# Local attention: sums of q k on VectorE, products p v on ScalarE, order of issue planned anew

## The chip, the core and the metric

The kernel runs on 1 core of one Trainium2 chip. The metric is the device time of one execution in microseconds (us). TensorE is PE in the profile's rows (PEld its weight loads), VectorE is DVE, ScalarE is ACT, GpSimd is POOL, SyncE is SP; SP and POOL issue the DMAs here (rows with a q, as SPq, are an engine's queue).

## The reference

B, H, S, D = 8, 8, 576, 64. Attention is computed twice, once on q, k, v averaged over groups of 4 tokens and repeated, once within a band of 7 neighbours; the sum goes through two matrices gated with each other, and two more matrices:

```
out_d = softmax(scale * mean4(q) mean4(k)^T) mean4(v)      # 144 x 144 per head
out_up = repeat(out_d, 4)
scores = where(|i - j| < 4, scale * q k^T, -1e9)
x = out_up + softmax(scores) v                             # 4608 tokens x 512
h = (x w1 * x w2) w3                                        # 512 -> 1024 -> 1024
out = h w_out                                               # 1024 -> 512
```

All in float32, the weights wider. TensorE works with each factor split into a high and a low float32r part, three matmuls for one product.

## The kernel before

*Work on TensorE.* `fold` multiplies w3 by w_out once (`accw`, line 408) and keeps it as `wphl`. Then come 12 chunks of 384 tokens (`moe`): for each of 8 features f two gates (`pab`, 12 matmuls each, lines 323 to 325), a copy by ScalarE (`a`, 1010), a product by VectorE (1012), a split in `gh` (ScalarE, 1017) and `gl` (VectorE, 1019), and `down` (`acc`, 9 matmuls with `wphl`). Only two banks hold `pab`, so TensorE stops when `a` comes late. Pooled attention (`pooled`, `quad`: `s_ps`, `t_ps`, `o_ps`) is spread between. The local attention of the first two batches goes through TensorE as well (`group_unit`).

*Local attention of the other six batches.* It is 18 units (`unit`), each half a chunk, 192 tokens: on 128 partitions (8 heads times 16 blocks of 36 tokens) 12 tokens of 64 elements each, 768 elements. For each of 7 offsets o, VectorE multiplies q by shifted k (`pr`, 863) and the 64 elements of each token are summed into `s_t` (by VectorE in one instruction, 876, or by ScalarE token by token, 873, two instructions each). After a softmax of small instructions, `s_t` multiplies shifted v into `pv` (VectorE, one instruction, 930, or ScalarE, 12 instructions, 922), and the seven `pv` are added into `xl` (VectorE, 940, or a DMA that adds, issued by POOL, 938). A transpose (944), the pooled part (951) and the split (957, 958) end the unit; two units make a chunk's `xh` and `xl`.

*Buffers.* `q_t` has one buffer (`q=1` in `BUFS`), `pr` three, `pv` three. k and v share three buffers `kv`; k of a unit, v of it, and so on take them in turn, so that k of a unit takes the buffer of v of two units before. The loads of `q_t` (842), k (846) and v (850) are issued by SyncE, in one queue with the pooled loads and the stores of `o_sb` (1039, 1041).

*Who does what.* `SHARE` sets it, by offset o, and for the added DMAs by place i in the order of adding:

```
SHARE = dict(qk_pool=(), qk_act=(2, 4), av_act=(3, 5), dma_add=(2, 4, 6))
others = [o for o in range(W) if o in share["av_act"]]
mine = [o for o in range(W) if o not in others]
while mine or others:
    order += mine[:1] + others[:1]
```

*Order.* Nothing runs where it is written. Each step is recorded by `add(engine, cost, ...)` with what it needs; `Plan.order` lists all steps from these costs (`dve_us`, `act_us`, `mm_us` and numbers in place), then shifts priorities by the tables `SHIFTS`, and the steps are emitted in that order, each engine working in order. A cost is a number for the planner alone, not a wait.

Of the kernel before, what the change touches and what calls it, by code (L numbers as in the profile page):

```python
# [15 lines left out]
ALU = mybir.AluOpType  # L16
# [6 lines left out]
SD = S // FAC  # L23
# [29 lines left out]
BUFS = dict(pr=3, pv=3, xl=2, xt=1, q=1, kv=3, w3=5, early_raw=4, early_wx=2, late_raw=3, late_wx=2, a=2,
            g=2, o=2, ab=2, acc=1, ps=3, p=1, pt=1, oup=2, vs=1, qks=1, x=2, s=3, gs=3, q4=2, k4=2, qn=2, vw=4, se=4, pte=1, xf=1)


SHARE = dict(qk_pool=(), qk_act=(2, 4), av_act=(3, 5), dma_add=(2, 4, 6))
# [9 lines left out]
AHEAD = 4  # L67

SHIFTS = [
    "gates.8.2:2 gates.9.5:-15.5",  # L70
    "down.0.1:-10 down.0.4:21.5 down.0.5:47.5 down.0.7:-65 down.1.1:-12 down.1.5:2 down.11.2:-4.5 down.2.0:-1"
    " down.2.2:-2 down.2.3:-11.5 down.2.4:-7.5 down.2.5:-46.5 down.3.2:-14.5 down.3.3:8.5 down.3.6:-11"
    " down.3.7:-29.5 down.4.4:-7 down.4.6:-10 down.5.4:14 down.6.4:-36 down.6.5:5 down.6.6:2.5 down.6.7:-52"
    " down.7.4:-19 down.7.7:1.5 down.8.4:3.5 down.8.5:74 down.9.2:3 down.9.3:-24 gate_block.0.0.0:-5.5"
    " gate_block.0.1.0:-21 gate_block.0.1.1:-15.5 gate_block.1.0.2:-20.5 gate_block.1.1.0:-26.5"
    " gate_block.1.1.2:-6.5 gates.0.0:-14 gates.0.1:-4 gates.0.2:-3.5 gates.0.5:-6 gates.1.1:1 gates.1.3:2"
    " gates.1.6:-2.5 gates.2.0:4.5 gates.2.1:-11.5 gates.2.2:2.5 gates.2.3:-3 gates.2.4:-3 gates.2.5:0.5"
    " gates.3.1:-7 gates.3.2:-30 gates.3.5:-31 gates.3.7:-16.5 gates.4.0:-20.5 gates.4.1:-29 gates.4.2:-14"
    " gates.4.4:1.5 gates.5.2:3.5 gates.5.3:0.5 gates.5.6:-3 gates.5.7:-1.5 gates.6.0:2 gates.6.2:-19.5 gates.6.3:-2"
    " gates.6.6:-1 gates.7.1:1.5 gates.7.6:-0.5 gates.8.3:2.5 gates.8.7:3 gates.9.6:-31.5 group_scores.0.2.0:4"  # L80
    " group_scores.0.2.1:3.5 group_scores.1.0.1:4.5 group_scores.1.1.0:-3 group_values.1:-14 group_values.2:3"
    " out_weight.3:-1 out_weight.4:3 out_weight.6:14 part.6.1:10.5 pooled.0:2.5 pooled.1:4.5 pooled.3:5.5"
    " pooled.4:3.5 pooled.6:11 pooled_sums.1:2.5 product.4.5:-6 product.7.0:7 product.7.1:4 quad.1.0:10.5"
    " quad.2.0:-6 quad.2.1:1 quad.3.0:-4.5 quad.3.1:-1 quad.4.0:1.5 quad.4.1:1 quad.6.0:0.5 quad.7.0:-7.5 rest.0:-1"
    " rest.1:-21.5 unit.11:-1 unit.13:1 unit.14:1 unit.16:1 unit.17:-4.5 unit.20:0.5 unit.21:2 unit.22:-0.5"
    " unit.23:7 unit.6:-1 unit.7:-0.5",
]

LOWS = dict(early=('ACT', 'ACT', 'DVE'), late=('ACT', 'DVE'))
# [176 lines left out]
def dve_us(n, fast=False):  # L266
    return n / 1920 + 0.155 if fast else n / 960 + 0.1
# [8 lines left out]


def mm_us(n):
    return n * 0.43e-3 + 0.0095


SWITCH = 0.19
# [2 lines left out]
def dma_us(n, add=False):  # L285
    return n / (180e3 if add else 320e3)
# [3 lines left out]
def tile_attention_moe(ctx: ExitStack, tc: tile.TileContext, q, kw, vw, qk4, v4, w1, w2, w3, wout, edge, out):  # L290
    nc = tc.nc
# [17 lines left out]
    soft = wpool.tile([128, 3, KEYS[2] + SD], F32, name="pexp")  # L309
# [5 lines left out]
    gates = [[wpool.tile([128, KT, 2, 512], F32R, name=f"w{w}a"), None, None] for w in (1, 2)]  # L315
# [15 lines left out]
    early, late = [], []  # L331
# [221 lines left out]
    def quad(b, qd, P, lq, hq, hpt):  # L553
# [32 lines left out]
            ex.append(e)  # L586

        t1 = add("DVE", 0.19, lambda: nc.vector.tensor_scalar(out=T["rs"][:, :nt], in0=T["sm"][:, :nt], scalar1=1e-9, scalar2=float(FAC), op0=ALU.add, op1=ALU.mult), ex, uses=[hg])
        rs = add("DVE", 0.12, lambda: nc.vector.reciprocal(T["rs"][:, :nt], T["rs"][:, :nt]), [t1], uses=[hg])
        no = []  # L590
        wide_ = lambda x, n: x.unsqueeze(2).to_broadcast([128, nt, n])
        width = (SD, 128)
        if b in PB:
            for par, i in slots:
                no.append(add("ACT", act_us(SD, 1), lambda par=par, i=i: nc.scalar.mul(out=T["of"][par][:, i, :width[par]], in_=T["of"][par][:, i, :width[par]], mul=T["rs"][:, i, par:par + 1]), [rs], uses=[hg, hp]))
        else:
            for par in range(2):
# [33 lines left out]
    @plan.named  # L631
    def pooled_sums(b):

        fours[b], four_ready[b] = {}, []
        hq, done = None, []
        for qd in range(2):
            fours[b][qd] = {}
            tq = hn = None
            for w in range(2):
                x = {}  # L640

                def load_q(qd=qd, w=w, x=x):
# [24 lines left out]
                done.append(t)
                pep.extend([lq4, tq])

            def load_k(qd=qd):  # L670
                x = fours[b][qd][1] = pools["pep"].tile([128, FAC, 2, SD], F32, name="k4", bufs=BUFS["k4"])
                for f in range(FAC):
                    nc.sync.dma_start(out=x[:, f], in_=qk4[b, f, :, 1, 2 * qd:2 * qd + 2])
            lk4, hk4 = add("SP", 2.0, load_k, take=[R["k4"]], late=dma_us(128 * 4608))
            t = lk4
            for f in range(1, FAC):
                def total(qd=qd, f=f):
                    to, x = raws[b][0][:, 1, 2 * qd:2 * qd + 2], fours[b][qd][1]
# [155 lines left out]
    def unit(n):  # L834
# [74 lines left out]
        for i, o in enumerate(order):  # L909
# [266 lines left out]
```

## Time and profile before

| | us |
|---|---|
| median of 3 runs | 773.48 (770.54 to 774.76) |
| profiled execution, its own time | 773.75 |
| its span | 771.9 |
| granted TensorE clock, mean | 0.994 |
| busy: PE / DVE / ACT / POOL | 739.4 / 618.3 / 525.5 / 153.2 |
| instructions | 14990 |

The span runs from the first to the last instruction of the profiled execution; matmuls overlap, so the sum of their durations is over PE's busy time. Waits are put down to what released the instruction last. The rows that matter are shown in the prediction.

### The profile page before, as it was taken

What the parts mean: (1) busy time and instruction counts of PE and PEld (TensorE: products, weight loads), DVE (VectorE), ACT (ScalarE), POOL (GpSimd) and SP (SyncE); (2) the same over time, 40 slices, a digit from 0 to 9 for tenths busy, and PEclk for the clock granted to TensorE, in tenths of its full rate; (3) what the DMA queues carried; (4) which work ended last, traced back from release to release, by engine and by line L of the source; (5) the groups of instructions that cost most, each with busy time, mean ns of one, the idle gap of its engine ahead of it and who ended that gap; (6) DMA issues with size and microseconds to landing.
All of it is one profiled execution on the core that took longest, in us unless ns stands there. A gap on an engine that the chain in (4) does not pass through costs nothing.

```text
span 771.9 us, 14990 instructions
## 1 busy us (share of the span) xinstructions
PE 739.4 (96%) x5248; PEld 640.1 (83%) x5248; DVE 618.3 (80%) x1076; ACT 525.5 (68%) x2074; POOL 153.2 (20%) x187
## 2 busy tenths in 40 slices
PE   3899989999999999999999999999999999999994
PEld 1345578789988999899998898999988998999994
DVE  5658886658999999999997999999989999973110
ACT  4679688547877787867787688677686886742211
POOL 1120033101012512141130422420223320110000
PEclk9999999999999999999999999999999999999998
DMA  9995768415349747877459668764569544331101
GB/s 313 307 285 168 229 176 202 86 42 186 68 115 239 148 109 210 165 147 174 106 132 209 99 158 221 135 169 110 124 150 224 121 100 123 80 65 20 42 1 41
DMA packets 46051, 111.91 MB, mean 145 GB/s; under 512 B 6280, under 2 KB 12424, under 8 KB 45976
## 3 DMA queue, kind: packets, MB, share of 16 engines
q0 software_dynamic: 15360, 38.94, 29.6%
q1 hardware_dynamic: 30616, 72.01, 28.6%
q8 instruction: 41, 0.67, 0.4%
q14 instruction: 34, 0.28, 0.1%
HBM read 80.26 MB, written 9.44 MB: 116 GB/s over the span
## 4 chain that ended last, share of the span: by engine, by line
PE 75%; DMA 9%; DVE 7%; ACT 5%; issue 3%; POOL 0%; SPq 0%; DVEq 0%; ACTq 0%; POOLq 0%
PE pab L323 15%; PE pab L325 15%; PE pab L324 15%; PE acc L323 7%; PE acc L325 7%; PE acc L324 7%; DMA raw<-in_w_dram 4%; DMA kv<-in_kw_dram 2%; DMA out_dram<-o_sb 2%; PE accw L408 2%; DVE pr L863 2%; PE o_ps L527 1%; PE s_ps L566 1%; PE t_ps L609 1%; DMA xl<-pv 1%
## 5 line engine op out<-in xcount | busy, mean ns | idle before, releaser
L873 ACT ACTIVATE junk<-pr 128x64 f32<-128x64 f32 x432 | 111.2, 257 | 23.8 <-DVE pr L863 12.8
L863 DVE TENSOR_TENSOR pr<-q_t,kv 128x768 f32<-128x768 f32 x126 | 119.6, 967 | 3.9 <-DMA kv<-in_kw_dram 3.5
L922 ACT ACTIVATE pv<-kv,s_t 128x64 f32<-128x64 f32 x432 | 111.0, 338 | 12.1 <-DVE s_t L899 6.5
L323 PE MATMUL acc<-wphl,gh 128*128 128x512 f32 x288 | 114.4, 397 | 0.0
L325 PE MATMUL acc<-wphl,gl 128*128 128x512 f32 x288 | 113.2, 393 | 0.9 <-DVE gl L1019 0.9
L324 PE MATMUL acc<-wphl,gh 128*128 128x512 f32 x288 | 112.7, 391 | 0.0
L938 POOL DMA_DIRECT2D xl<-pv x54 | 48.4, 896 | 300.5 <-DVE xl L940 211.8
L1010 ACT COPY a<-pab 128x384 f32<-128x384 f32 x96 | 45.8, 477 | 70.5 <-PE pab L325 54.7
L1012 DVE TENSOR_TENSOR a<-pab,a 128x384 f32<-128x384 f32 x96 | 53.1, 553 | 48.4 <-PE pab L325 46.4
L876 DVE TENSOR_REDUCE s_t<-pr 128x12 f32<-128x768 f32 x90 | 84.1, 946 | 0.4
L873 ACT ACTIVATION_READ_ACCUMULATOR junk<-pr 128x1 f32 x432 | 81.2, 188 | 0.0
L1017 ACT CAST gh<-a 128x384 fp32r<-128x384 f32 x96 | 48.9, 509 | 45.1 <-PE acc L324 38.9
L1019 DVE TENSOR_TENSOR gl<-a,gh 128x384 fp32r<-128x384 f32 x96 | 54.2, 566 | 27.5 <-ACT gh L1017 25.9
L408 PE MATMUL accw<-wo,w 128*128 128x512 f32 x128 | 62.1, 621 | 14.4 <-DVE w L370 13.3
L930 DVE TENSOR_TENSOR pv<-kv,s_t 128x768 f32<-128x768 f32 x72 | 69.6, 969 | 0.1
L323 PE MATMUL pab<-xh,wb 128*128 128x384 f32 x192 | 66.1, 344 | 2.1 <-ACT a L1010 2.1
L323 PE MATMUL pab<-xh,w1a 128*128 128x384 f32 x192 | 65.9, 343 | 2.1 <-ACT a L1010 1.6
L323 PE MATMUL pab<-xh,wo 128*128 128x384 f32 x192 | 65.9, 343 | 0.3 <-ACT a L1010 0.3
L323 PE MATMUL pab<-xh,w2a 128*128 128x384 f32 x192 | 65.2, 340 | 0.5 <-DVE a L1012 0.5
L325 PE MATMUL pab<-xh,wb 128*128 128x384 f32 x192 | 65.2, 339 | 0.0
L324 PE MATMUL pab<-xl,wb 128*128 128x384 f32 x192 | 65.2, 339 | 0.0
L324 PE MATMUL pab<-xl,w1a 128*128 128x384 f32 x192 | 64.9, 338 | 0.3
(117 smaller groups left out, 1717.2 us busy)
## 6 DMA issues: line engine op xcount, KB each, us to landing
xl<-pv POOLq DMA_DIRECT2D x54, 384.0 KB, 4.3
raw<-in_w_dram SPq DMA_DIRECT2D x32, 512.0 KB
qks<-in_qk_dram POOLq DMA_DIRECT2D x18, 576.0 KB, 7.3
kv<-in_kw_dram SPq DMA_DIRECT2D x18, 576.0 KB
kv<-in_vw_dram SPq DMA_DIRECT2D x18, 576.0 KB
q_t<-in_q_dram SPq DMA_DIRECT2D x18, 384.0 KB
out_dram<-o_sb SPq DMA_DIRECT2D x24, 256.0 KB
raw<-in_wout_dram SPq DMA_DIRECT2D x8, 512.0 KB
```

The lines of the kernel that those rows point to most:

```text
L323: nc.tensor.matmul(out_ps, lhsT=lh, rhs=rh, start=first, stop=False)
L324: nc.tensor.matmul(out_ps, lhsT=lh, rhs=rl, start=False, stop=False)
L325: nc.tensor.matmul(out_ps, lhsT=ll, rhs=rh, start=False, stop=last)
L408: nc.tensor.matmul(accs[m], lhsT=T["x"][:, j % 4 * 128:j % 4 * 128 + 128], rhs=wo[0][:, j], start=j == 0, stop=j == NF - 1)
L863: (nc.gpsimd if o in share["qk_pool"] else nc.vector).tensor_tensor(out=T[o], in0=T["q"], in1=T["k"][:, o * D:o * D + nq].rearrange("p (t ...
L873: nc.scalar.activation(out=junk, in_=T[o][:, t], func=AF.Copy, accum_out=T["s"][:, t, o:o + 1])
L876: reds.append(add("DVE", dve_us(nq), lambda o=o: nc.vector.tensor_reduce(out=T["s"][:, :, o], in_=T[o], op=ALU.add, axis=AX.X), [tp], uses ...
L922: nc.scalar.mul(out=T["pv", o][:, tt], in_=T["v"][:, (tt + o) * D:(tt + o + 1) * D], mul=T["s"][:, tt, o:o + 1])
L930: nc.vector.tensor_tensor(out=T["pv", o], in0=T["v"][:, o * D:o * D + nq].rearrange("p (t d) -> p t d", d=D), in1=T["s"][:, :, o].unsqueez ...
L1012: tg = add("DVE", dve_us(CT), lambda f=f: nc.vector.tensor_tensor(out=T["a", f], in0=T["p", 1, f], in1=T["a", f], op=ALU.mult), [ta, ends[ ...
L1017: nc.scalar.copy(out=T["gh", f], in_=T["a", f])
L1019: tl = add("DVE", dve_us(CT), lambda f=f: nc.vector.tensor_tensor(out=T["gl", f], in0=T["a", f], in1=T["gh", f].bitcast(F32), op=ALU.subtr ...
```

## The change

Per unit, VectorE takes all seven sums of q k (ScalarE did those of o = 2 and 4). Of the seven products p v ScalarE takes five (o = 1, 2, 3, 5, 6; before 3 and 5), VectorE two (0 and 4). Two adds go by DMA instead of three, at places 2 and 5, so VectorE adds four instead of three. `q_t` gets a second buffer. Some costs of the planner change, and the tables that shift the order are new, so all engines' orders are.

```
-BUFS = dict(pr=3, pv=3, xl=2, xt=1, q=1, kv=3, ...
+BUFS = dict(pr=3, pv=3, xl=2, xt=1, q=2, kv=3, ...
-SHARE = dict(qk_pool=(), qk_act=(2, 4), av_act=(3, 5), dma_add=(2, 4, 6))
+SHARE = dict(qk_pool=(), qk_act=(), av_act=(1, 2, 3, 5, 6), dma_add=(2, 5))
 SHIFTS = [
-    "gates.8.2:2 gates.9.5:-15.5",
+    "group_scores.0.1.0:-3",
...
 def mm_us(n):
-    return n * 0.43e-3 + 0.0095
+    return n * 0.432e-3 + 0.0098
...
-        rs = add("DVE", 0.12, lambda: nc.vector.reciprocal(...
+        rs = add("DVE", 0.16, lambda: nc.vector.reciprocal(...
-                no.append(add("Pool", 0.18 + nt * width[par] * 2.4e-3, ...
+                no.append(add("Pool", 0.32 + nt * width[par] * 2.4e-3, ...
-        no.append(add("DVE", dve_us(nt * KR), ...
+        no.append(add("DVE", dve_us(nt * KR) + 0.17, ...
-                    tq, hn = add("DVE", dve_us(4 * SD), turn, ...
+                    tq, hn = add("DVE", 0.58, turn, ...
-                    t = add("Pool", 0.9, lambda o=o: nc.gpsimd.dma_start(out=T["x"], in_=T["pv", o], accum_op=ALU.add), ...
+                    t = add("Pool", 0.83, lambda o=o: nc.gpsimd.dma_start(out=T["x"], in_=T["pv", o], accum_op=ALU.add), ...
```

Lines behind the shift tables stand one line higher in the changed kernel. Three places of the order follow; numbers behind names are those of the buffers' tiles.

SyncE's queue at the tenth local unit (the one whose k load the trace shows at 407 us). Before: its q is `q_t_5016`, its k `kv_5047`, its v `kv_5054`; `vs` and `vl` are loads of the pooled v.

```order
L1041 DMA out_0_dram<-o_sb_4907 8x16x512
L1041 DMA out_0_dram<-o_sb_4957 4x16x512 x2
L1041 DMA out_0_dram<-o_sb_4997 8x16x512
L842 DMA q_t_5016<-in_q_dram 128x768
L846 DMA kv_5047<-in_kw_dram 128x1152
L850 DMA kv_5054<-in_vw_dram 128x1152
L490 DMA vs_5112<-in_v4_dram 72x512
L491 DMA vs_5112<-in_v4_dram 56x512
L492 DMA vl_5113<-in_v4_dram 16x512
```

After: its k is `kv_5166`, its v `kv_5172`; `q_t_5125` is the q of the eleventh unit.

```order
L1040 DMA out_0_dram<-o_sb_4950 8x16x512
L1040 DMA out_0_dram<-o_sb_4974 4x16x512 x2
L1040 DMA out_0_dram<-o_sb_5015 8x16x512
L841 DMA q_t_5125<-in_q_dram 128x768
L489 DMA vs_5138<-in_v4_dram 72x512
L490 DMA vs_5138<-in_v4_dram 56x512
L491 DMA vl_5139<-in_v4_dram 16x512
L845 DMA kv_5166<-in_kw_dram 128x1152
L849 DMA kv_5172<-in_vw_dram 128x1152
```

The load of q moved one unit ahead; k and v of the unit moved behind the pooled v.

ScalarE's queue at the products of the eighth local unit, whose v gives up the buffer for that k. Before: v is `kv_4403`, and VectorE's product `pv_5035` is the last one that reads it.

```order
L922 ACTIVATE pv_4773<-kv_4403,s_t_4488 128x64 x6
L922 ACTIVATE pv_4841<-kv_4403,s_t_4488 128x64 x6
L581 ACTIVATE pexp_77,gsm_4807<-s_ps_4809,gnb_4806 128x144 x3
L581 ACTIVATE pexp_77,gsm_4807<-s_ps_4810,gnb_4806 128x144
L1017 CAST gh_4874<-a_4771 128x384
L581 ACTIVATE pexp_77,gsm_4807<-s_ps_4810,gnb_4806 128x144 x2
L1010 COPY a_4888<-pab_4790 128x384
L922 ACTIVATE pv_4841<-kv_4403,s_t_4488 128x64 x4
L1028 COPY o_sb_4907<-acc0_4371 128x512
L922 ACTIVATE pv_4841<-kv_4403,s_t_4488 128x64 x2
L873 ACTIVATE junk_74,s_t_4800<-pr_4877 128x64 x2
```

After: v is `kv_4451`, `pv_5120` is the fifth product of ScalarE.

```order
L921 ACTIVATE pv_5033<-kv_4451,s_t_4553 128x64 x6
L615 COPY pt_4856<-t_ps_5036 128x6x64
L615 COPY pt_4856<-t_ps_5040 128x6x64
L617 COPY pt_4856<-t_ps_5044 128x12x16
L921 ACTIVATE pv_5033<-kv_4451,s_t_4553 128x64 x6
L921 ACTIVATE pv_5120<-kv_4451,s_t_4553 128x64 x8
L539 COPY oup_5144<-o_ps_5086 128x2x9x16
L539 COPY oup_5144<-o_ps_5091 128x2x9x16
L921 ACTIVATE pv_5120<-kv_4451,s_t_4553 128x64 x4
L1016 CAST gh_5161<-a_4909 128x384
L890 ACTIVATE s_t_4870<-s_t_4870 128x84
```

The last reader of v moved from VectorE to ScalarE, up to the exponential (890) of the next unit.

VectorE's queue where the first local unit begins. Before (products `pr`, sums `s_t`; 1019 and 1012 belong to the gates):

```order
L863 TENSOR_TENSOR pr_2290<-q_t_2237,kv_2221 128x768
L876 TENSOR_REDUCE s_t_2289<-pr_2290 128x12
L863 TENSOR_TENSOR pr_2315<-q_t_2237,kv_2221 128x768
L863 TENSOR_TENSOR pr_2326<-q_t_2237,kv_2221 128x768
L1019 TENSOR_TENSOR gl_2313<-a_2268,gh_2312 128x384
L863 TENSOR_TENSOR pr_2339<-q_t_2237,kv_2221 128x768
L1012 TENSOR_TENSOR a_2328<-pab_2319,a_2328 128x384
L876 TENSOR_REDUCE s_t_2289<-pr_2315 128x12
```

After:

```order
L862 TENSOR_TENSOR pr_2265<-q_t_2214,kv_2212 128x768
L875 TENSOR_REDUCE s_t_2264<-pr_2265 128x12
L862 TENSOR_TENSOR pr_2283<-q_t_2214,kv_2212 128x768
L862 TENSOR_TENSOR pr_2291<-q_t_2214,kv_2212 128x768
L1011 TENSOR_TENSOR a_2281<-pab_2274,a_2281 128x384
L862 TENSOR_TENSOR pr_2300<-q_t_2214,kv_2212 128x768
L875 TENSOR_REDUCE s_t_2264<-pr_2283 128x12
L875 TENSOR_REDUCE s_t_2264<-pr_2291 128x12
L875 TENSOR_REDUCE s_t_2264<-pr_2300 128x12
```

Each `pr` is now summed by VectorE. From the first `pr` to the second `xl` split (958, now 957), which completes the first chunk of local units, VectorE's queue holds 72 instructions of 768 elements before and 79 after.

More of the change, by code (lines that the diff above doesn't have):

```diff
@@ L50 @@
 NG = UN // GQ
[L53 removed]
+BUFS = dict(pr=3, pv=3, xl=2, xt=1, q=2, kv=3, w3=5, early_raw=4, early_wx=2, late_raw=3, late_wx=2, a=2,
             g=2, o=2, ab=2, acc=1, ps=3, p=1, pt=1, oup=2, vs=1, qks=1, x=2, s=3, gs=3, q4=2, k4=2, qn=2, vw=4, se=4, pte=1, xf=1)
[L57 removed]
+SHARE = dict(qk_pool=(), qk_act=(), av_act=(1, 2, 3, 5, 6), dma_add=(2, 5))
 TOKENS = 2
@@ L69 @@
 SHIFTS = [
-    "gates.8.2:2 gates.9.5:-15.5",
[L71 to L86, printed above, removed]
[16 rows of a table added]
 ]
@@ L588, in quad @@
         t1 = add("DVE", 0.19, lambda: nc.vector.tensor_scalar(out=T["rs"][:, :nt], in0=T["sm"][:, :nt], scalar1=1e-9, scalar2=float(FAC), op0=ALU.add, op1=ALU.mult), ex, uses=[hg])
-        rs = add("DVE", 0.12, lambda: nc.vector.reciprocal(T["rs"][:, :nt], T["rs"][:, :nt]), [t1], uses=[hg])
+        rs = add("DVE", 0.16, lambda: nc.vector.reciprocal(T["rs"][:, :nt], T["rs"][:, :nt]), [t1], uses=[hg])
         no = []
@@ L597, in quad @@
             for par in range(2):
-                no.append(add("Pool", 0.18 + nt * width[par] * 2.4e-3, lambda par=par: nc.gpsimd.tensor_tensor(out=T["of"][par][:, :, :width[par]], in0=T["of"][par][:, :, :width[par]], in1=wide_(T["rs"][:, :nt, par], width[par]), op=ALU.mult), [rs], uses=[hg, hp]))
-        no.append(add("DVE", dve_us(nt * KR), lambda: nc.vector.tensor_tensor(out=soft[:, :nt, KEYS[1]:KEYS[2]], in0=T["of"][1][:, :, 128:], in1=wide_(T["rs"][:, :nt, 1], KR), op=ALU.mult), [rs], uses=[hg, hp]))
+                no.append(add("Pool", 0.32 + nt * width[par] * 2.4e-3, lambda par=par: nc.gpsimd.tensor_tensor(out=T["of"][par][:, :, :width[par]], in0=T["of"][par][:, :, :width[par]], in1=wide_(T["rs"][:, :nt, par], width[par]), op=ALU.mult), [rs], uses=[hg, hp]))
+        no.append(add("DVE", dve_us(nt * KR) + 0.17, lambda: nc.vector.tensor_tensor(out=soft[:, :nt, KEYS[1]:KEYS[2]], in0=T["of"][1][:, :, 128:], in1=wide_(T["rs"][:, :nt, 1], KR), op=ALU.mult), [rs], uses=[hg, hp]))
         pts = []
@@ L651, in pooled_sums @@
                 if w == 0:
-                    tq, hn = add("DVE", dve_us(4 * SD), turn, [lq4], take=[R["qn"]], uses=[hq4])
+                    tq, hn = add("DVE", 0.58, turn, [lq4], take=[R["qn"]], uses=[hq4])
                 else:
-                    tq = add("DVE", dve_us(4 * SD), turn, [lq4, tq], uses=[hq4, hn])
+                    tq = add("DVE", 0.58, turn, [lq4, tq], uses=[hq4, hn])
                 t = lq4
@@ L937, in unit @@
                 if i in share["dma_add"]:
-                    t = add("Pool", 0.9, lambda o=o: nc.gpsimd.dma_start(out=T["x"], in_=T["pv", o], accum_op=ALU.add), [t, tm], uses=[hx, h], late=dma_us(128 * nq * 4, True))
+                    t = add("Pool", 0.83, lambda o=o: nc.gpsimd.dma_start(out=T["x"], in_=T["pv", o], accum_op=ALU.add), [t, tm], uses=[hx, h], late=dma_us(128 * nq * 4, True))
                 else:
```

15 rows, old and new, of the table SHIFTS are left out of this document.

## The prediction

> **What bounds the kernel now.** I read the page's busy shares first, then busy time by stage, then the waits and the chain of waits inside the one stage where something stops, and last the groups of instructions that the change touches.
>
> ```profile
> PE 739.4 (96%) x5248; PEld 640.1 (83%) x5248; DVE 618.3 (80%) x1076; ACT 525.5 (68%) x2074; POOL 153.2 (20%) x187
> ...
> 0.00:60.00 60.00, 44.99 (x233) 19.58 (x233) 34.56 (x86) 37.12 (x83) 11.25 (x28) 1.00 0.95 304
> 60.00:180.00 120.00, 115.66 (x1425) 89.67 (x1424) 89.18 (x221) 87.16 (x295) 19.94 (x23) 1.00 0.58 157
> 180.00:680.00 500.00, 496.63 (x3171) 454.99 (x3170) 470.63 (x735) 381.05 (x1653) 119.48 (x133) 1.00 0.63 144
> 680.00:760.00 80.00, 80.00 (x417) 74.51 (x416) 23.98 (x37) 18.40 (x42) 2.58 (x3) 1.00 0.12 25
> 760.00:771.90 11.90, 2.08 (x10) 1.38 (x8) 0.00 (x0) 1.76 (x3) 0.00 (x0) 0.77 0.24 66
> ```
>
> After each stretch and its length stand the busy times of PE, PEld, DVE, ACT and POOL, then granted clock, DMA share and GB/s. PE is the bound. What it lacks of the span is 32.5 us: 15.0 in the first 60 us, where the DMA share is 0.95; 4.3 from 60 to 180; 3.4 in the whole of 180 to 680, where the local attention runs; nothing from 680 to 760; 9.8 in the tail. The change keeps all 5248 matmuls, so it can gain only by taking stops of PE away. VectorE, at 470.6 of 500 us in the local stage, is next: when it stops, PE soon does.
>
> The waits of PE from 180 to 680 are two rows, and the longest piece has a chain that can be read in order of time:
>
> ```profile
> PE pab L323 <- ACT a L1010: 2.3, 3, 1.8
> PE acc L325 <- DVE gl L1019: 0.9, 1, 0.9
> ...
> 404.99 1.75 DVE pr L863 x2
> ...
> 406.76 0.66 SPq L842
> ...
> 407.47 15.15 DMA kv<-in_kw_dram
> ...
> 407.47 2.48 SPq L846 DMA_DIRECT2D kv<-in_kw_dram  x1
> ...
> 422.71 0.96 DVE L863 TENSOR_TENSOR pr<-q_t,kv 128x768 f32<-128x768 f32 x1 [3.49 <-DMA kv<-in_kw_dram]
> ...
> 426.29 0.45 DVE gl L1019
> ...
> 426.76 0.49 ACT a L1010
> ...
> 427.29 0.44 PE pab L323
> ```
>
> Unit by unit: the last product of a unit (404.99) frees the only `q_t`; SyncE, in order, issues the next `q_t` (406.76), only then `kv` with k; k takes 15.15 us, VectorE stops 3.49 us in front of its next product, `gl` and `a` are late, PE stops 1.8 us. It costs more than the stop:
>
> ```profile
> 425.00:428.00 3.00, 1.16 (x6) 0.74 (x6) 3.00 (x6) 1.24 (x4) 1.63 (x3) 1.00 0.67 127
> 428.00:431.00 3.00, 3.00 (x13) 3.00 (x12) 3.00 (x5) 1.95 (x9) 2.27 (x3) 0.59 0.63 80
> 431.00:434.00 3.00, 3.00 (x16) 3.00 (x15) 2.53 (x5) 2.81 (x16) 0.90 (x2) 0.84 0.37 57
> ```
>
> 1.84 us idle, then a granted clock of 0.59 and 0.84: 3 x 0.41 + 3 x 0.16 = 1.7 us of matmul time lost. One such stop is worth 3.5 us. The Trainium skill, TensorE: Matmul & The Clock Gate, What's actually happening, says the clock falls back after an idle window of about 3.4 us; by it a stop of 1.84 us costs 1.84 and no more. The trace differs: 0.59 after 1.84 us.
>
> **The change part by part.** There are 18 local units. These groups carry it (busy us, mean ns of one):
>
> ```profile
> L863 DVE TENSOR_TENSOR pr<-q_t,kv 128x768 f32<-128x768 f32 x126 | 119.6, 967 | 3.9 <-DMA kv<-in_kw_dram 3.5 <-ACT junk L873 0.4
> L873 ACT ACTIVATE junk<-pr 128x64 f32<-128x64 f32 x432 | 111.2, 257 | 23.8 <-DVE pr L863 12.8
> L922 ACT ACTIVATE pv<-kv,s_t 128x64 f32<-128x64 f32 x432 | 111.0, 338 | 12.1 <-DVE s_t L899 6.5 <-DMA xl<-pv 5.3
> L876 DVE TENSOR_REDUCE s_t<-pr 128x12 f32<-128x768 f32 x90 | 84.1, 946 | 0.4
> ...
> 402.72 0.55 DVE L1012 TENSOR_TENSOR a<-pab,a 128x384 f32<-128x384 f32 x1
> 403.19 0.94 DVE L876 TENSOR_REDUCE s_t<-pr 128x12 f32<-128x768 f32 x1
> ...
> 406.65 1.80 DVE L876 TENSOR_REDUCE s_t<-pr 128x12 f32<-128x768 f32 x2
> 408.38 0.94 DVE L930 TENSOR_TENSOR pv<-kv,s_t 128x768 f32<-128x768 f32 x1
> 409.24 0.96 DVE L944 STREAM_TRANSPOSE xt<-xl 128x768 f32<-128x768 f32 x1
> ...
> 402.06 0.26 ACT L873 ACTIVATE junk<-pr 128x64 f32<-128x64 f32 x1
> 402.22 0.19 ACT L873 ACTIVATION_READ_ACCUMULATOR junk<-pr 128x1 f32 x1
> 402.44 0.26 ACT L873 ACTIVATE junk<-pr 128x64 f32<-128x64 f32 x1
> ...
> 415.18 1.55 ACT L922 ACTIVATE pv<-kv,s_t 128x64 f32<-128x64 f32 x6
> ```
>
> Instructions overlap, so I cost them from start to start: a wide VectorE instruction of 768 elements 0.87 us (two reduces from 406.65 to 408.38; product 408.38 to 409.24), one of 128x384 0.47 (402.72 to 403.19), a sum of one token on ScalarE 0.38 (402.06 to 402.44), a product of one token 0.24 ((1.55 - 0.34) / 5).
>
> - VectorE: two more sums per unit, +36 x 0.87 = +31.3; three products fewer (of five), -54 x 0.87 = -47.0; adds four instead of three, +18 x 0.87 = +15.7. Sum 0.0.
> - ScalarE: -432 x 0.38 = -164.2, +648 x 0.24 = +155.5. Sum -8.7. It is idle a third of the span; worth nothing by itself.
> - POOL and DMA: adds by DMA go from 54 to 36.
>
> ```profile
> q0 software_dynamic: 15360, 38.94, 29.6%
> q1 hardware_dynamic: 30616, 72.01, 28.6%
> ...
> xl<-pv POOLq DMA_DIRECT2D x54, 384.0 KB, 4.3
> ```
>
> 18 x 384 KB = 7.1 of the 38.9 MB of q0, 18% of its 29.6%: the DMA share of the span falls by 5.4 points. No engine waits for bytes on average; it counts only where a load lands late.
>
> - `q_t` in two buffers: a load no longer waits for the last product of the unit just ahead of its own. But in the new order each `q_t` load stands one unit earlier, so the last product of a unit still gates the `q_t` load that SyncE has ahead of the next k; behind that wait stand k and v of the next unit and, at some units, the pooled v. The 3 KB per partition that it needs cost no time.
> - k's own buffer: with three buffers in the ring k and v take turns, and k of a unit takes the buffer that v of two units before gives up. VectorE's last product gave it up before; now ScalarE's twelfth token of the fifth product does, shortly ahead of use.
>
> The sum, stage by stage. At the stop of 425 the issue of k ended at 407.47 + 2.48 = 409.95, and VectorE could have used it at 422.71 - 3.49 = 419.2, 9.3 us later. In the new order, at the same unit, between ScalarE's last token of the freeing product and the first product stand on VectorE 7 wide instructions, 4 of 128x384 and four small: 6.1 + 1.9 = 8.0, some 9 with the small. That is the same lead, on queues with 5 points less on them. Between all of the stop staying (0) and all of it going (-3.5) I take the middle: -1.8. The other PE stops of the stage:
>
> ```profile
> 300.00:360.00 60.00, 59.65 (x379) 54.04 (x378) 55.89 (x89) 45.05 (x189) 18.75 (x21) 1.00 0.77 170
> 560.00:600.00 40.00, 38.84 (x271) 34.35 (x270) 36.45 (x61) 29.92 (x126) 13.37 (x16) 1.00 0.81 184
> ...
> 570.88 7.69 DMA xl<-pv
> ```
>
> 0.35 + 1.16 = 1.5 us, the larger one behind an add by DMA that took 7.69 us. With a third fewer adds, in less traffic, I take two thirds away: -1.0 (between 0 and -1.5).
>
> A new place is the first chunk that the local units feed. Up to its second `xl` the new order puts 79 wide instructions on VectorE where there were 72, +7 x 0.87 = +6.1 us, because sums that ScalarE did beside it stand in its queue now. The reserve before was:
>
> ```profile
> 264.53 0.95 DVE L958 TENSOR_TENSOR xl<-xt,xh 128x768 fp32r<-128x768 f32 x1
> ...
> 271.09 0.33 PE L323 MATMUL pab<-xh,w1a 128*128 128x384 f32 x1
> ```
>
> 265.5 to 271.1, 5.6 us. PE's own work ahead of it stays nearly the same (six `pab` matmuls more, three `acc` fewer), and waits of VectorE for ScalarE's sums there go. Nearly even: +0.3 (between 0 and +3, a stop with its slow clock).
>
> Fold and gate weights, 0 to 180 us: order planned anew, the same loads (a weight load or two change places with a load of v). Of the 19.3 us of idle there the larger part lies where the DMA share is 0.95, and the bytes are the same; I see no term of either sign and take 0 (between -2 and +2). From 680 on PE is full, and the tail is the same three copies and stores: 0.
>
> -1.8 - 1.0 + 0.3 = -2.5. The profiled execution took 773.75 us (span 771.9 and 1.85 around it), 0.27 over the median, so the sum is set against the median 773.48: **771.0**. By the skill's clock rule the term of 425 would be half of 1.84, and the forecast 771.9.
>
> **The rivals.** A measurement of this kernel tells about 0.5% from no change (the three runs span 770.54 to 774.76); that puts the borders at 769.6 and 777.4.
>
> *All late stops go.* Less traffic, no ScalarE sums ahead of the softmax and a k that lands in time remove the 3.5 and 1.5, and the new order of the gate weights half of the 4.3 us of 60 to 180: 773.5 - 5.0 - 2.2 = 766.3. For it: all are waits, not work. Against it: the lead of k is no longer than before.
>
> *k arrives late at several units (the slow side).* ScalarE's five products take 5 x 12 x 0.24 = 14.4 us a unit, cut up by `a`, `gh`, `oup` and exponentials, and only then is v's buffer free for k of the unit after next. If the load takes 10 us or more against a lead of under 10, VectorE stops, and each stop like that of 425 costs 3.5. From two more stops than I have counted (771.0 + 7.0 = 778.0) the kernel is slower; with three it takes 781.5. For it: the landing of 15.15. Against it: only one stop in 18 units before, with a lead no longer.
>
> *Stops are worth their length alone* (the clock rule above, or stops that move elsewhere): 771.9 to 773.5, no change. The 0.59 speaks against the first.
>
> **How the numbers follow.** The forecast 0.45 (768.5 to 773.5; 0.08 of it below 769.6), all late stops go 0.32, stops worth their length or moved 0.05, late k 0.18. Faster 0.08 + 0.32 = 0.40; the same 0.37 + 0.05 = 0.42; slower 0.18. Range: down to 764, the second case with the 2 us of the first 180 us on top; up to 779, the late k with two stops and a bit of the first chunk's.
>
> **What would show it.** In the changed kernel: DVE busy near 618 and ACT some 10 us of real time lower; `xl<-pv` 36 times; PE idle in 180 to 680 at about 2 us rather than 3.4, no granted clock of 0.91 around 420 to 440; `pr` waiting for `kv` under 2 us in all; first chunk of the local units without a stop over 1 us. The prediction is wrong if `pr` waits for `kv` at three or more units, if PE idle before 180 us moves by over 2 us, or if matmuls of one shape take another pace.

## The result, and the profile after

The changed kernel is slower, by 0.7%: 779.39 us median of 20 runs (773.42 to 785.46, and one of 2568.1) against 773.57 us of 20 runs of the kernel before. The ratio is 1.007, 95% interval 1.0047 to 1.0093, and leaves out the two slow runs of 785.46 and 2568.1. The profiled execution took 780.05 us, its span is 778.3, mean clock 0.991; before 773.75, 771.9 and 0.994.

The page of the changed kernel, busy shares and two rows of its DMA part (queue and issues):

```profile
PE 742.9 (95%) x5248; PEld 641.2 (82%) x5248; DVE 619.6 (80%) x1076; ACT 538.0 (69%) x1858; POOL 132.7 (17%) x169
...
q0 software_dynamic: 12768, 31.86, 24.0%
...
xl<-pv POOLq DMA_DIRECT2D x36, 384.0 KB, 4.4
```

Busy time by stage, with the columns of the prediction's first fence:

```profile
0.00:60.00 60.00, 43.93 (x226) 18.73 (x227) 33.91 (x84) 35.39 (x80) 11.65 (x28) 0.97 0.90 290
60.00:180.00 120.00, 116.13 (x1404) 88.98 (x1404) 86.89 (x215) 85.99 (x286) 17.81 (x21) 0.99 0.59 163
180.00:680.00 500.00, 494.19 (x3162) 451.29 (x3161) 470.63 (x735) 382.09 (x1389) 100.67 (x117) 1.00 0.55 129
680.00:760.00 80.00, 80.00 (x420) 74.87 (x419) 27.05 (x43) 31.81 (x99) 2.56 (x3) 1.00 0.14 31
760.00:778.30 18.30, 8.64 (x43) 7.34 (x41) 1.12 (x2) 2.75 (x5) 0.00 (x0) 0.88 0.16 43
```

VectorE's work is that of before (619.6 against 618.3, and 470.63 in the local stage both times). The 6.4 us of span are two things. PE is idle 35.4 us instead of 32.5: +1.1 in the first 60 us, -0.5 from 60 to 180, +2.4 from 180 to 680, -0.2 in the tail. And the same 5248 matmuls are busy 3.5 us longer, which fits the granted clock: two slices of 20 us that were at 1.00 before are at 0.91, 1.8 us each. In the local stage one slice is at 0.91 in both kernels (500 to 520 here, 420 to 440 before):

```profile
40.00:60.00 20.00, 19.35 (x128) 8.70 (x129) 11.61 (x26) 16.07 (x40) 5.30 (x6) 0.91 0.86 251
80.00:100.00 20.00, 17.96 (x157) 9.30 (x155) 13.65 (x35) 12.26 (x31) 1.89 (x3) 0.91 0.78 243
500.00:520.00 20.00, 18.04 (x89) 16.99 (x89) 15.56 (x28) 14.47 (x53) 2.63 (x3) 0.91 0.59 135
```

What stops VectorE and PE, from the waits of the changed kernel (us in total, times, longest):

```profile
PE accw L407 <- DVE w L369: 15.6, 5, 8.3
...
DVE xl L939 <- DMA xl<-pv: 7.9, 4, 3.8
DVE pv L929 <- DMA xl<-pv: 4.3, 2, 2.5
...
ACT pv L921 <- DMA xl<-pv: 1.4, 1, 1.4
...
PE pab L322 <- ACT a L1009: 4.2, 7, 2.0
PE pab L322 <- DVE a L1011: 2.5, 1, 2.5
PE oe_ps L791 <- DMA v_w<-in_v_dram: 2.0, 1, 2.0
```

The same waits in the kernel before:

```profile
PE accw L408 <- DVE w L370: 13.3, 4, 8.4
...
ACT pv L922 <- DMA xl<-pv: 5.3, 5, 2.2
...
DVE xl L940 <- DMA xl<-pv: 2.6, 1, 2.6
```

No product `pr` waits for a load of k any more. But 36 adds by DMA are waited for 13.6 us (3.0 of them behind 680 us, where PE is full), where 54 were waited for 7.9 us before (2.6 by VectorE, 5.3 by ScalarE). In the early part PE waits 2.3 us longer for VectorE's weights `w` of `fold`, and 2.0 us for the load `v_w`. The chain of waits at the two worst places (start, length, what):

```profile
501.30 0.52 POOL vs L488
501.82 7.95 DMA xl<-pv
...
509.79 0.04 DVE pv L929
...
510.66 0.96 DVE xl L939
...
512.30 0.40 ACT gh L1016
...
513.18 0.39 ACT a L1009
...
513.61 0.44 PE pab L322
...
588.28 0.51 POOL qks L504
588.79 9.51 DMA xl<-pv
...
598.32 0.97 DVE xl L939
...
600.22 0.53 DVE a L1011
...
600.79 0.45 PE pab L322
```

Each add stands in POOL's queue behind pooled loads that add (`vs`, `qks`), takes 8.0 and 9.5 us to land, VectorE stands still, and the copy or product `a` that frees PE's bank is late.

### The profile page after: what moved, and what is told of

Same layout as the page of the kernel before. It is cut to its first block, busy times and chain, and to the rows that moved or that the text cites. A ratio compares the mean times of both kernels' runs of the same rounds, so it can differ in the third digit from the quotient of the medians.

```text
span 778.3 us, 14740 instructions
## 1 busy us (share of the span) xinstructions
PE 742.9 (95%) x5248; PEld 641.2 (82%) x5248; DVE 619.6 (80%) x1076; ACT 538.0 (69%) x1858; POOL 132.7 (17%) x169
## 4 chain that ended last, share of the span: by engine, by line
PE 66%; DMA 15%; issue 6%; DVE 5%; ACT 4%; POOL 2%; SPq 1%; POOLq 0%; ACTq 0%; DVEq 0%
PE pab L322 13%; PE pab L324 13%; PE pab L323 13%; PE acc L322 7%; PE acc L324 6%; PE acc L323 6%; DMA xl<-pv 4%; DMA raw<-in_w_dram 4%; PE accw L407 2%; DMA vl<-in_v_dram 2%; PE o_ps L526 1%; DMA raw<-in_wout_dram 1%; PE s_ps L565 1%; DMA out_dram<-o_sb 1%; DVE xl L939 1%
## 5 line engine op out<-in xcount | busy, mean ns | idle before, releaser
L921 ACT ACTIVATE pv<-kv,s_t 128x64 f32<-128x64 f32 x1080 | 276.2, 340 | 21.3 <-DVE xl L939 11.8
L875 DVE TENSOR_REDUCE s_t<-pr 128x12 f32<-128x768 f32 x126 | 115.6, 946 | 0.2
L937 POOL DMA_DIRECT2D xl<-pv x36 | 32.5, 904 | 303.4 <-DVE xl L939 158.8
L407 PE MATMUL accw<-wo,w 128*128 128x512 f32 x128 | 66.1, 652 | 16.1 <-DVE w L369 15.6
L939 DVE TENSOR_TENSOR xl<-xl,pv 128x768 f32<-128x768 f32 x72 | 68.6, 954 | 8.8 <-DMA xl<-pv 7.9
L322 PE MATMUL pab<-xh,wb 128*128 128x384 f32 x192 | 65.9, 343 | 3.8 <-DVE a L1011 2.5
L322 PE MATMUL pab<-xh,w1a 128*128 128x384 f32 x192 | 66.0, 344 | 2.3 <-ACT a L1009 2.3
L322 PE MATMUL pab<-xh,wo 128*128 128x384 f32 x192 | 65.8, 343 | 0.6 <-ACT a L1009 0.6
L322 PE MATMUL pab<-xh,w2a 128*128 128x384 f32 x192 | 65.6, 342 | 0.0
L324 PE MATMUL pab<-xh,w1a 128*128 128x384 f32 x192 | 65.3, 340 | 0.0
L324 PE MATMUL pab<-xh,w2a 128*128 128x384 f32 x192 | 64.8, 338 | 0.0
L323 PE MATMUL pab<-xl,w2a 128*128 128x384 f32 x192 | 64.8, 338 | 0.0
L324 PE MATMUL pab<-xh,wo 128*128 128x384 f32 x192 | 64.7, 337 | 0.0
```

What stands on the lines that cost most here:

```text
L322: nc.tensor.matmul(out_ps, lhsT=lh, rhs=rh, start=first, stop=False)
L323: nc.tensor.matmul(out_ps, lhsT=lh, rhs=rl, start=False, stop=False)
L324: nc.tensor.matmul(out_ps, lhsT=ll, rhs=rh, start=False, stop=last)
L407: nc.tensor.matmul(accs[m], lhsT=T["x"][:, j % 4 * 128:j % 4 * 128 + 128], rhs=wo[0][:, j], start=j == 0, stop=j == NF - 1)
L875: reds.append(add("DVE", dve_us(nq), lambda o=o: nc.vector.tensor_reduce(out=T["s"][:, :, o], in_=T[o], op=ALU.add, axis=AX.X), [tp], uses ...
L921: nc.scalar.mul(out=T["pv", o][:, tt], in_=T["v"][:, (tt + o) * D:(tt + o + 1) * D], mul=T["s"][:, tt, o:o + 1])
```

## The experiments

All ratios are to the kernel before, run together with the kernel at hand, with 95% intervals. The expectations say "sums by DMA" for the adds by DMA. Theory A is that late adds make the loss behind 180 us, theory B that the early order makes the loss. Where adds are left out (their products are computed, but not added) or moved, the lines are those of `unit`, around 937.

**The adds by DMA left out of the changed kernel**

```
-  lambda o=o: nc.gpsimd.dma_start(out=T["x"], in_=T["pv", o], accum_op=ALU.add)
+  lambda o=o: None
```

> The changed kernel with the 36 sums by DMA left out: two of the seven products p v are computed and not added to the output tile; all else is issued in the same order. Theory A (the loss after 180 us comes from sums by DMA that land late, VectorE stops 12.2 us on them): VectorE's stops on xl<-pv are gone, the idle time of TensorE from 180 to 680 us falls from 5.8 to at most 3 us, and the time from 779.4 to 773.5 to 775.5. Rival (the shifted division of work itself, VectorE with all seven products q k and ScalarE with five products p v, is too slow for TensorE): 779, within 1 us. If the early part (theory B) carries the whole loss: 779 too.

Measured 772.18 us, ratio 0.9992 (0.9964 to 1.002). The local stage:

```profile
180.00:680.00 500.00, 499.44 (x3208) 458.09 (x3208) 474.36 (x745) 388.65 (x1414) 71.44 (x84) 1.00 0.41 105
```

PE's idle time there goes from 5.81 to 0.56 us, as theory A had it. The adds cost the changed kernel 0.0078, 6.0 us.

**The control: the kernel before without its adds** (same edit)

> The kernel before with its 54 sums by DMA left out (three of seven products p v are computed and not added); the control for the changed kernel without its 36. If the sums by DMA cost the kernel before nearly nothing (VectorE stopped 2.6 us on them there) and the changed one 6 us: ratio to before 0.997 to 1.000, 770 to 772.3. If they cost both kernels alike, as the same DMA load does: 0.990 to 0.993, 765 to 767, and then the changed kernel's loss is not theirs.

Measured 767.18 us, ratio 0.9924 (0.9896 to 0.9951): 0.0076. This is the second case of the expectation. The adds are dear in both kernels, and theory A in its plain form, that the adds as a group make the difference, falls: without any add the changed kernel is still 0.0068 behind. A third fewer adds saved nothing that the runs can tell (0.0002 dearer, good to about 0.004).

**Five of the adds moved to VectorE**, in the version with the early order of the kernel before (next but one):

```
+ON_DVE = {(10, 5), (11, 5), (16, 5), (19, 2), (19, 5)}      # unit, place
-  lambda o=o: nc.gpsimd.dma_start(...)
+  lambda o=o, i=i: nc.vector.tensor_tensor(out=T["x"], in0=T["x"], in1=T["pv", o], op=ALU.add) if (n, i) in ON_DVE else nc.gpsimd.dma_start(...)
```

> The changed kernel with the order of the kernel before ahead of the first local chunk, and five of the 36 sums by DMA (those that VectorE or ScalarE stood waiting for in the trace of the changed kernel: the second sum of the chunks at 332, 356, 502 and 589 us and the first at 576 us) taken by VectorE in the same place of the order. All is computed. Late sums as the cause: the stops at 511 and 590 us go, ratio 0.999 to 1.001, 771.5 to 773, against 1.005 with the sums by DMA. If VectorE cannot take 5 x 0.95 us more: 1.005 or above, with new stops of TensorE at these chunks.

Measured 772.55 us, 0.9992 (0.9964 to 1.002), against 1.005 with them on DMA. VectorE takes the extra work, and PE's idle time in the local stage is 2.13 us, 1.3 of it at the seam:

```profile
180.00:680.00 500.00, 497.87 (x3183) 455.76 (x3182) 476.45 (x742) 387.51 (x1408) 96.51 (x112) 1.00 0.53 127
```

So five late adds of 36 carry 0.0058 of the 0.0079 that all of them cost in this version (1.005 against 0.9971 without any, below). Five adds that nobody waits for were not moved as a control.

**Two adds earlier in POOL's queue**

```
     order = plan.order()
+    for moved, behind in ((2575, 2389), (2573, 2575), (2574, 2573), (2919, 2736)):
+        order.remove(plan.tasks[moved])
+        order.insert(order.index(plan.tasks[behind]) + 1, plan.tasks[moved])
```

> The changed kernel; on POOL's queue alone the sum by DMA that was issued at 501.8 us stands ahead of the last three accumulating loads of vl and vs, and the one issued at 588.8 us ahead of the accumulating load of qks that waited 6.4 us. Theory A with POOL's order as the reason that the sums land late: the stops of VectorE of 2.5 us at 507 us and of 3.8 us at 594 us go, TensorE's idle time there (about 1.0 at 511 us, 4.5 at 598 us) and the slow clock behind it too, and the time is 774.5 to 776. Rival (they land late because the DMA engines are loaded then, whatever the order of issue): the sums are issued earlier and land as late, 778.5 to 779.5. Rival (division of work): 779.

Measured 783.89 us (6 runs), 1.0148 (1.0101 to 1.0194): slower, which no theory had. (PE's two stops, which the expectation gives as 1.0 and 4.5 us, are 1.96 and 2.51 us in the profile.) By stages of the profile:

```profile
340.00:360.00 20.00, 18.37 (x93) 16.20 (x93) 18.70 (x24) 15.79 (x57) 1.75 (x2) 1.00 0.42 104
500.00:520.00 20.00, 17.52 (x101) 16.12 (x100) 16.12 (x29) 12.35 (x44) 4.35 (x5) 0.95 0.64 142
580.00:600.00 20.00, 19.82 (x158) 17.42 (x157) 18.67 (x29) 17.15 (x64) 5.37 (x7) 1.00 0.96 223
```

The stop at 590 is gone (PE idle 0.18 of 20 us instead of 1.89): the add now lands in 5.1 us instead of 9.5, so there POOL's queue was the reason. At 500 the add holds nobody any more either, it lands in 4.0 us instead of 7.95. But PE idles 2.48 us instead of 1.96, for another load: `vl`, which now stands behind the add, is issued at 504.71 and lands at 509.74, ScalarE waits for it, and VectorE waits for ScalarE's exponential.

```profile
ACT vl L510 <- DMA vl<-in_v_dram: 4.0, 1, 4.0
...
510.71 0.24 DVE L894 TENSOR_REDUCE sm<-s_t 128x12 f32<-128x84 f32 x1 [3.05 <-ACT s_t L890]
```

So the edit cured both adds, and at one place the load that it put back became the late transfer. A stop of 1.6 us at 340 us is new, behind an add that the edit doesn't touch; the waits have it as

```profile
DVE pv L929 <- DMA xl<-pv: 4.3, 1, 4.3
```

Why the runs are slower than the profile's stops explain stays open.

**The early order of the kernel before in the changed kernel**, all that is issued ahead of the first local chunk:

```
+HEAD = [int(x) for x in (
...
     order = plan.order()
+    head = [plan.tasks[i] for i in HEAD]
+    order = head + [t for t in order if t not in set(head)]
```

> The changed kernel, but all that is issued ahead of the first local chunk (weights, folds, the first pooled batches) stands in the order of the kernel before. Two causes together (2.5 us lost ahead of 180 us, 3.8 us behind): 777, idle time of TensorE from 0 to 180 us about 19.4 us as before instead of 19.9, and without the slow clock at 80 to 100 us. All of the loss behind 180 us: 779.4. All of it ahead of 180 us: 773.6.

Measured 775.03 us, 1.005 (1.002 to 1.008). The early order would be worth 0.002 of the 0.007 by it, within the noise; the slow clock at 80 to 100 us is gone, and PE idles 17.1 us ahead of 180 us instead of 19.9.

**The reverse: the early order of the changed kernel in the kernel before** (the same edit with the other list)

> The kernel before, but all that is issued ahead of the first local chunk stands in the order of the changed kernel; the division of the products and sums is that of the kernel before. Two causes together: 776. All of the loss behind 180 us: 773.6. All of it ahead of 180 us: 779.4.

Measured 781.27 us (6 runs), 1.0116 (1.0063 to 1.0168), more than any theory. The halves were planned for each other, and PE has new stops at the seam (1.9 us from 140 to 160, 1.8 from 180 to 200), so this number is not the early order alone. Of the two swaps only the first was worth following, and it has a seam too:

```profile
180.00:200.00 20.00, 18.72 (x98) 17.04 (x97) 18.98 (x31) 7.88 (x28) 0.00 (x0) 1.00 0.29 90
```

**The same without adds**

> The changed kernel with the order of the kernel before ahead of the first local chunk, and without its sums by DMA (two of seven products not added): what is left of the change is the division of work, the second buffer of q and the order of the local stage. Two causes (late sums, early order) and nothing else: within 1.5 us of the kernel before without its sums, and about 2 us below the changed kernel without its sums (ratio 0.9992), so 0.996 to 0.998. If the division of work costs TensorE time by itself: above 1.000.

Measured 771.61 us, 0.9971 (0.9941 to 1.0000): within the two-cause range, but 0.0047 above the kernel before without its adds, where 1.5 us were allowed.

**The seam mended**

```
+    for moved, behind in ((755, 1048), (756, 755), (770, 769), (1050, 770)):
+        order.remove(plan.tasks[moved])
+        order.insert(order.index(plan.tasks[behind]) + 1, plan.tasks[moved])
```

> The changed kernel with the early order of the kernel before, and at the seam (181 to 187 us) one subtraction gl and one product a taken by VectorE ahead of the three reductions and the product q k that made TensorE stop there for 1.3 us. If the new early order is the loss (TensorE some 5 us behind at 180 us) and the division of work costs nothing: TensorE does not stop at 180 to 200 us and the ratio is 1.000 to 1.003. If the division of work or the local stage is the loss: 1.005 or above, as without the mending.

Measured 776.31 us, 1.0059 (1.0033 to 1.0085); PE's idle time from 180 to 200 us falls from 1.28 to 0.46, the time doesn't. By the expectation the early order is not the main part of the loss.

```profile
180.00:200.00 20.00, 19.54 (x102) 17.58 (x101) 18.52 (x31) 7.61 (x24) 0.00 (x0) 1.00 0.29 90
```

Its waits for adds:

```profile
DVE xl L977 <- DMA xl<-pv: 10.9, 5, 3.6
DVE pv L967 <- DMA xl<-pv: 2.1, 2, 1.7
```

VectorE waits 13.0 us for adds there: the late ones came with the local order.

**Mended, with the five adds on VectorE; mended, without adds**

> The same, and five of the 36 sums by DMA taken by VectorE, which gave -0.0058 and -0.0065 in two other versions. If that adds up again: 0.994 to 0.998, faster than both kernels. If the mending and the sums hide each other: 0.999.

Measured 771.97 us, 0.9994 (0.9966 to 1.0023): -0.0065 from the five adds, but not faster than the kernel before.

> The changed kernel with the early order of the kernel before, the seam mended, and without its 36 sums by DMA (two of seven products not added). If the division of work and the order behind 180 us are free by themselves: 0.992 to 0.995, as the kernel before without its sums (0.9924). If they cost TensorE 3 us or more by themselves: 0.997 or above, as with the seam.

Measured 769.9 us, 0.9957 (0.9931 to 0.9983), between the two cases, 0.0033 above the kernel before without adds; the intervals overlap.

**One early stop taken away**

```
     order = plan.order()
+    order.remove(plan.tasks[117])
+    order.insert(order.index(plan.tasks[116]) + 1, plan.tasks[117])
```

> The changed kernel; on SyncE's queue alone one load of v_w (four transfers) stands ahead of eight transfers of k instead of behind them. In the trace of the changed kernel TensorE waited 2.04 us for that load at 84.8 us, and the slice of 80 to 100 us ran at clock 0.91. If the order of the first 180 us costs the time by such stops and by the slow clock behind them: the stop goes, the slice is at 1.00, and the time falls by 2 to 4 us, ratio to the kernel before 1.002 to 1.004 against 1.007. If the early stops are absorbed later: 1.007.

Measured 777.7 us, 1.0067 (1.004 to 1.0094). The slices:

```profile
40.00:60.00 20.00, 17.02 (x107) 7.64 (x107) 12.39 (x28) 16.17 (x42) 5.02 (x6) 1.00 0.88 258
80.00:100.00 20.00, 17.96 (x176) 9.69 (x174) 15.61 (x39) 12.10 (x32) 2.51 (x3) 1.00 0.82 256
```

The wait for `v_w` and the slow clock are gone, but PE idles the same 2.04 us in 80 to 100 (1.4 of it now for VectorE's `xf`) and 2.98 instead of 0.65 in 40 to 60. The stop moved; the runs gained nothing.

> The same, and in addition the five sums by DMA that were waited for in the trace of the changed kernel are taken by VectorE (all is computed). If the early stop and the late sums are two causes that add up: 1.007 less 0.003 to 0.005 less 0.0058 (what the five sums gave with the other early order): 0.996 to 0.999, 770 to 772.5. If one hides the other: 0.999 to 1.002.

Measured 773.96 us, 1.0002 (0.9975 to 1.0028): -0.0065 by the adds again, the load gave nothing.

**A second look at each kernel**

> The kernel before once more, for a second profile. The prediction's first term rests on one stop, at 425 us (a load of k late by 3.5 us, TensorE idle 1.84 us). If that stop belongs to the kernel: it is there again, and the slice of 420 to 440 us is slow again. If it belongs to that one execution: VectorE does not wait for k there, and TensorE idles in 180 to 680 us for other sums or loads, 1 to 4 us in all.

One run, 770.15 us. VectorE doesn't wait for k (of the loads and adds of the local units, it waits 5.4 us for adds alone), and there is no slow slice at 420:

```profile
420.00:440.00 20.00, 20.00 (x119) 18.34 (x118) 19.71 (x31) 14.47 (x66) 8.70 (x11) 1.00 0.60 111
```

The stop on which the first term rested belonged to that execution, not to every one.

> The changed kernel once more, for a second profile. If the loss of the early order belongs to the kernel: TensorE's busy time behind 180 us is again 580 us or more (the kernel before had 578.7 and 575.2 in two executions), idle about 20 us ahead of 180 us, with a slice at 0.91 at 40 or 80 us. If the stops at 511 and 598 us belong to the kernel: VectorE waits again for sums by DMA at both. If they belong to that execution: it waits at other sums.

One run, 779.15 us. Ahead of 180 us PE idles 20.6 us (15.9 in the second execution of the kernel before), and 40 to 60 is at clock 0.83. PE's busy time behind 180 us is 584.6 us (582.8 in the first execution, 578.7 and 575.2 before), so the early loss belongs to the kernel, as the expectation has it. The stop at 590 us is there again (VectorE waits 2.4 us for the add issued at 589 us), that at 511 only with 0.9 us. In the local stage PE idles 3.45 us, against 3.29 in the second execution of the kernel before: this pair lost its time ahead of 180 us and not behind.

**q in two buffers alone, and k and v in four**

```
-  T["q"] = ...tile([128, UT, D], F32, name="q_t", bufs=BUFS["q"])
+  T["q"] = ...tile([128, UT, D], F32, name="q_t", bufs=2)
```

> The kernel before with q in two buffers, its order unchanged: one part of the change alone. No load of q was waited for in the trace before behind 180 us, so 0.998 to 1.002. If earlier loads of q take DMA time from the sums by DMA or from k: above 1.002.

Measured 773.76 us, 1.0021 (0.9993 to 1.0048): no difference. The late k at 425 us is back, in the waits (first) and with its slow clock by stage (second):

```profile
DVE pr L863 <- DMA kv<-in_kw_dram: 4.4, 1, 4.4
```

```profile
420.00:440.00 20.00, 17.26 (x95) 15.73 (x95) 16.55 (x21) 12.31 (x58) 9.27 (x11) 0.91 0.51 87
```

So the buffer of q, with the old order, doesn't help k.

```
-  name="kv", bufs=BUFS["kv"]        # 3
+  name="kv", bufs=4
```

> The kernel before with the tile of k and v in four buffers instead of three, order unchanged: the load of k that came late at 425 us can start when the load ahead of it is issued. If the buffer held it: the stop of VectorE of 3.5 us and the idle 1.84 us of TensorE with its slow slice at 420 to 440 us go, ratio 0.995 to 0.997, 769 to 770. If the queue or the DMA engines held it: 1.000.

Measured 772.94 us, 0.9987 (0.9956 to 1.0018). The stop at 425 is absent, as in one run with three buffers, and the time is the same.

**The late adds of the kernel before on VectorE** (the edit of the five, with six adds, then ten)

> The kernel before, with six of its 54 sums by DMA taken by VectorE in the same place of the order: those of its trace that took 7.7 to 8.9 us to land and that VectorE or ScalarE waited for (at 412, 471, 509, 571, 587 and 617 us). All is computed. Leaving out all 54 gave 0.9924. If the few late ones carry the cost of them all, as in the changed kernel: 0.994 to 0.997, 768 to 770. If the cost is spread, or comes through the load of k at 425 us: 0.999 to 1.000.

Measured 771.77 us, 0.9971 (0.9945 to 0.9998).

> The kernel before with ten of its 54 sums by DMA on VectorE instead of six: those that were waited for in any of its profiles. All is computed. Six gave 0.9971, all 54 left out 0.9924. If the late sums carry the cost: 0.994 to 0.997. If VectorE's 3.8 us more eat it up: 0.998 to 1.000.

Measured 772.1 us, 0.9975 (0.9951 to 0.9999). Both are some 2 us faster than the kernel before, by intervals that end just under 1; four more adds on VectorE gave nothing more. Six late adds carry 0.0029 of the 0.0076 that all 54 cost here. Where the rest lies is not shown.

## Why the prediction was wrong

The forecast was 2.5 us less than before, and the kernel became 5.8 us slower. The step that failed is the costing of the adds by their number (-1.0), and with it two others: the early order, put at nothing, and a stop at 425 us that only some executions have (-1.8). The pairs side by side, ratios to the kernel before:

| | adds by DMA as they are | the late ones on VectorE | left out |
|---|---|---|---|
| kernel before | 1 | 0.9971 | 0.9924 |
| changed, early order of before, seam mended | 1.0059 | 0.9994 | 0.9957 |
| changed kernel | 1.007 | 1.0002 (with the early `v_w`) | 0.9992 |

Read along the right column, the gap of 0.0102 between the forecast (771.0 to 773.48, 0.9968) and 1.007 is 0.0035 for the early order, 0.0033 for what is left, 0.0023 for the stop at 425 if nothing came of it, 0.0015 for the adds as a group, less 0.0004 for the first local chunk. Differences of two ratios are good to about 0.004, so this tells where the gap can lie and does not prove the shares.

- *Adds, -1.0: the step that failed with its sign.* "With a third fewer adds, in less traffic, I take two thirds away" counted adds. The column of those left out shows 0.0076 for 54 and 0.0078 for 36, and PE's idle time in the local stage, forecast at about 2 us, was 3.5 to 5.8 us in five executions with the new local order and 2.6 to 4.2 in four with the old order throughout. Traffic did fall (DMA share in the local stage 0.63 to 0.55), and an add lands no sooner. POOL's adds into `xl`, before (first) and after (second):

```profile
DMA to landing us min/median/max: 3.9/4.3/10.1
```

```profile
DMA to landing us min/median/max: 3.9/4.4/9.5
```

  What costs most in the changed kernel is the few that land after their user is ready, and those follow the order, not the number: in the same five executions (all adds on DMA and POOL's order as planned), VectorE waits 2.4 to 3.8 us for the same add, issued at 583 to 589 us. The middle column shows that the late ones can be had apart: moving five gave 0.0058 to 0.0065 in three versions of the changed kernel, moving six or ten gave 0.0029 and 0.0025 in the kernel before. By these numbers the late ones became dearer by some 0.0035 (2.7 us) and the others cheaper by as much. Such differences of differences are good to 0.003 at best: the first is at the edge of the noise, the second is not shown.
- *The stop at 425, -1.8: mechanism right, size wrong.* `pr` waits for `kv` in none of the twelve executions with the new local order, and in five of eight with the old one (0.7 to 4.4 us). But the stop of 3.5 us or more came in the first profile and in the one with two q buffers, not in the second profile of before. A price of 3.5 us that only some executions pay was set against a median over all of them, and half was still too much.
- *The first 180 us, 0: outside its bounds of ±2 by the traces, its size not settled by the runs.* "I see no term of either sign" went by bytes and left out which load comes when. The first pair of profiles puts 4.2 us there (0.6 idle, two slices of 1.8 slow clock), the second pair 4.7 us of idle time and more slow clock. Over all the runs here, PE idles 15.9 to 19.5 us ahead of 180 us in 13 executions with the old early order (17.8 on average) and 19.9 to 23.0 in seven with the new one (20.8). The ranges don't meet, and the averages differ by 3.0 us. By the table's last two rows the early order is worth 0.0008 to 0.0035, 0.6 to 2.7 us (the middle pair differs by the `v_w` load too). Early stops move when one is taken away, so the term is not one stop.
- *What is left.* 0.0033 (2.5 us) between the first two rows without adds is the division of work, the new local order and the mended seam together, and it may be nothing: the intervals overlap. Division of work as a cause was not shown. VectorE's balance of 0.0 was right. ScalarE's was not: instead of -8.7 us its busy time rose by 12.5 (525.5 to 538.0), as a token's product took 0.26 us and not 0.24, and a token's sum had taken 0.35 and not 0.38. It had room; VectorE waits only 0.6 us for its products at the adds.
- *First local chunk, +0.3.* PE has no stop from 260 to 280 us in either execution of the changed kernel; the term was small and right.
- *The slow rival* ended on the right side with the wrong mechanism: in both executions of the changed kernel k never came late. The late transfer was the add, a step that the prediction had booked as a gain alone.
- *The price of a stop.* 3.5 us for 1.84 idle was taken as a rule. At 598 us a longer stop cost its length alone (below).

Of the list of what would show it, DVE near 618, 36 adds, `pr` not waiting for `kv`, a clock of 1.00 from 420 to 440 and the absent stop at the first chunk held. ScalarE's 10 us less and PE's 2 us of idle time in 180 to 680 (5.81) did not, and the slow slice of the stage was at 500 to 520 instead. "PE idle before 180 us moves by over 2 us" didn't occur in the first pair (0.6), which hid that the slow clock had taken 3.6 us there; in the second pair it did (4.7).

## What to carry to other kernels

A group of transfers is not worth its number or bytes: find those whose user waits, in more than one execution, and move these first; in the changed kernel five of 36 were worth two thirds to four fifths of all, in the kernel before six of 54 some 40%. Before a forecast rests on a single stop, look at a second profile of the same kernel, since a stop that depends on when a load lands comes and goes. And a new order must be costed over the whole kernel, in granted clock as well as idle time: here its early part, costed at nothing, idles PE 3 us more on average, and the slow clock comes on top.

## What the runs showed of the hardware

A stop of PE has no fixed price. In the changed kernel, stages of 3 us around its two stops (1.96 and 2.51 us in one piece):

```profile
511.00:514.00 3.00, 1.04 (x6) 0.71 (x5) 3.00 (x5) 2.29 (x7) 0.87 (x1) 1.00 0.00 0
514.00:517.00 3.00, 3.00 (x13) 3.00 (x12) 3.00 (x5) 1.96 (x9) 0.00 (x0) 0.59 0.91 145
517.00:520.00 3.00, 3.00 (x17) 3.00 (x16) 1.88 (x3) 2.91 (x12) 0.00 (x0) 0.84 0.36 85
...
597.00:600.00 3.00, 1.28 (x6) 0.72 (x4) 1.64 (x2) 0.00 (x0) 0.78 (x1) 1.00 0.70 167
600.00:603.00 3.00, 2.21 (x13) 2.21 (x14) 2.97 (x5) 1.37 (x4) 1.69 (x2) 1.00 0.28 35
603.00:606.00 3.00, 3.00 (x15) 2.46 (x14) 3.00 (x5) 2.21 (x8) 1.37 (x3) 1.00 0.39 64
```

The shorter one is followed by clocks of 0.59 and 0.84 (matmuls of `pab` start 0.32 us apart there instead of 0.17), the longer one by 1.00. The Trainium skill, TensorE: Matmul & The Clock Gate, What's actually happening, says that the windows run freely and that where a burst falls in them varies from run to run; that fits two stops with two prices, but not a fall after 1.96 us of idle time where the page gives a window of about 3.4 us.

An add of 384 KB by DMA never landed in under 3.9 us, and in 8.0 and 9.5 us at the two stops, where it stood in POOL's queue behind pooled loads that add; moved ahead of them, the same two landed in 4.0 and 5.1 us. The Trainium skill, DMA: Bandwidth & Descriptors, Anatomy of one DMA, fits a transfer issued by POOL as 2.0 us plus its bytes at 436 GB/s; the estimate from that is 2.9 us for an add, a third less than the median of 4.3 to 4.4 that the trace shows, and the trace decides.
